# S4D convolution and gMLP on one core: stacked parameters in six rows, no tensor_scalar among them, the last inverse stage in four tiles, a new order

## The chip, the cores and the metric

The kernel runs on one core of one Trainium2 chip. The metric is the device time of one execution in microseconds (us). Smaller is better.

## The reference

```python
# u [1, 2048, 512]; A = -exp(log_A_real) + 1j*A_imag, C = C_real + 1j*C_imag: 512 channels x 128 modes
dt = exp(log_dt); P = exp((A * dt)[:, :, None] * arange(2048))
K = 2 * einsum("dn,dnl->dl", C * dt, P).real
y = irfft(rfft(layernorm(u), 4096) * rfft(K, 4096))[:2048]      # along the sequence
h = u + y + layernorm(u) * D_skip
z = gelu(layernorm(h) @ w_in)                                    # 512 -> 1792
z1, z2 = z[:, :896], layernorm(z[:, 896:])
out = h + (z1 * (w_sp @ z2 + b_sp[:, None])) @ w_out             # w_sp 2048 x 2048
```

## The kernel before

**Phase A** (0 to 302.7 us of the profiled execution) makes the convolution. `phase_a` writes its operations into a list (`Plan`): `RANKS` holds two digits in base 64 for each operation and so gives the order of issue, `FORMS` says which of two engines takes an operation that was written with `nc.either`, and `BANKS` names the PSUM bank of each intermediate. So the order on PE, DVE (VectorE), ACT, POOL (GpSimd) and on SP's DMA queue is a table, not the text. All operations of the list have one line in the profile, L252 (`Plan.issue`); they are told apart by their tiles.

The 512 channels go in four chunks of 128. `load_params` and `params(al, c0, n, rt)` make the discretised parameters, for the chunks 0, 1 and then 2 and 3 together: |C_imag| and |C_real|, the angle by Arctan and Sin, three phase terms that are split into a high part and a remainder (the low part), all in the tile `trio` (later `big`), with the PSUM bank `a` between. These six rows go to DRAM (`scr_stk`), from where `stack(c, h)` reads them back into `sw`, spread over 128 partitions so that a product with the constant `c_k` gives the phases. In `scr_stk` there are 16 rows a mode: the six rows at 0, the same six at 10, and four rows of ones between, which four DMAs (`marks`) write from `c_one` at the start. `table(c, h)` makes the decay tables `mt` on POOL (three multiplies, an Exp on ACT, a multiply by the weights). The eight `unit`s of a chunk turn phases and tables into the kernel K in its first transform stage (`ps<-c_k,sw`, `f`, `wa`, `wb`, `ks`); `st1` and `piece_c` continue it. `norm_small` and `norm_x` are the layer norm of the input (BATCH_NORM_STATS2 on `big`); `piece_a`, `piece_b` and `exchange` transform it. `piece_d` (`ps<-big,a`) is the second stage of K's transform, followed on DVE by the multiplication with the spectrum (`trio<-ps,trio`); it goes in eight pieces of four 128-wide matmuls, each over all 32 of the last index. `piece_e` (`ps<-c_inv,trio`) is the first inverse stage, eight pieces, copied to `big`.

**Phase B1** (from 302.7) is written in order by hand (L901 to L964). `lines(n, ...)` is the last inverse stage for a quarter n of the channels, in groups of four lines into PSUM banks `y`: quarter 0 uses two 64x64 tiles of TensorE (L755), the others four (L763). `put_by` copies a group to SBUF (`stash`, L775), `add` adds it to the residual `xq` (from PSUM for quarter 0, L783; from `stash` otherwise, L780). `moments` takes statistics (L787), `centre` and `spread` combine them over partitions by small products with `c_mean` (`lnh_pm` L796, `lnh_pv` L810), `root` is 1/sqrt on DVE (L815 to L824). `by_halves` (L863) normalises and transposes the first quarter into `ht` in two halves; `column` (L877) is the product with w_in, for quarter 0 first over a first half of the rows (A), then over the second (B).

**Phases B2 and B3** make z2's layer norm, the product with w_sp in seven products in the manner of Strassen, the gate and w_out.

## Time and profile before

| | us |
|---|---|
| median of three runs (lowest, highest) | 851.99 (851.52, 867.98) |
| the profiled execution | 850.38 |
| its span | 848.4 |
| mean granted TensorE clock in it | 0.990 |
| PE busy | 772.8 (91%) |
| DVE busy | 620.0 (73%) |
| ACT busy | 449.1 (53%) |
| POOL busy | 281.5 (33%) |

PE is the time of matmuls, PEld that of loading their weights, which overlaps it. A row of a timeline gives the start, the length, the engine (a q behind it: its queue of DMAs), the line, the operation, output<-inputs with shapes and types, and how many were drawn together; in brackets the idle time before it and what ended that. The columns of the table by stretches stand with the prediction.

### The profile page before, as it was taken

The numbers are of one execution on the slowest core, as the hardware profiler recorded it, in microseconds if no ns is written. First come the engines' busy times: TensorE is split into PE (matmuls) and PEld (weight loads), VectorE is DVE, ScalarE is ACT, GpSimd is POOL, SyncE is SP. The second block draws the span as 40 slices with busy tenths as digits, with TensorE's granted clock in tenths as the row PEclk, the third lists the DMA queues.
The fourth block names the chain that finished last, engine by engine and source line by source line (L and its number), as shares of the span: only waits on it lengthen the run. The fifth ranks groups of instructions, "written<-read, shape, count | busy, mean of one in ns | idle before, by whom it ended". The sixth has DMA issues, their size and how long they took to land.

```text
span 848.4 us, 19968 instructions
## 1 busy us (share of the span) xinstructions
PE 772.8 (91%) x8081; PEld 658.5 (78%) x8081; DVE 620.0 (73%) x1187; ACT 449.1 (53%) x785; POOL 281.5 (33%) x334
## 2 busy tenths in 40 slices
...
GB/s 234 142 144 120 123 88 133 84 78 40 127 3 208 278 97 127 132 143 149 88 146 127 1 124 123 190 237 210 195 207 210 167 148 187 155 234 232 185 107 79
DMA packets 73515, 123.14 MB, mean 145 GB/s; under 512 B 6864, under 2 KB 29520, under 8 KB 72144
## 3 DMA queue, kind: packets, MB, share of 16 engines
...
q14 instruction: 28, 0.23, 0.1%
...
## 4 chain that ended last, share of the span: by engine, by line
PE 63%; ACT 2%; DVE 1%; issue 0%; DVEq 0%; ACTq 0%
PE m L1197 33%; PE pz L992 9%; PE pz L887 8%; PE po L1120 7%; PE pl L1120 2%; PE ps L252 2%; PE y L763 1%; PE y L755 1%; ACT w1r L835 1%; ACT ht L844 0%; ACT stash L775 0%; PE lnh_pv L810 0%; PE lnh_pm L796 0%; DVE w1r L842 0%; DVE w1r L833 0%
## 5 line engine op out<-in xcount | busy, mean ns | idle before, releaser
L1197 PE MATMUL m<-wts,zc_wa 128*128 128x512 f32 x700 | 221.1, 395 | 0.0
L1197 PEld LDWEIGHTS m<-wts,zc_wa 128*128 128x128 f32 x700 | 131.7, 188 | 31.0
L1197 PE MATMUL m<-wts,zc_wb 128*128 128x512 f32 x350 | 138.0, 394 | 0.0
L1068 POOL DMA_DIRECT2D raws<-in_w_sp_dram x64 | 58.1, 1010 | 214.0 <-DMA raws<-in_w_sp_dram 212.5
L252 POOL TENSOR_TENSOR wa<-mt 128x512 f32<-128x512 f32 x96 | 106.5, 1129 | 34.3 <-PE ps L252 23.4
L687 ACT CAST wts<-raws 128x512 fp32r<-128x512 f32 x112 | 68.8, 619 | 47.3 <-DMA raws<-in_w_sp_dram 21.0
L688 DVE TENSOR_TENSOR wts<-raws,wts 128x512 fp32r<-128x512 f32 x112 | 77.2, 691 | 18.7 <-ACT wts L687 18.3
L1197 PEld LDWEIGHTS m<-wts,zc_wb 128*128 128x128 f32 x350 | 65.8, 188 | 15.6
L992 PE MATMUL pz<-w,ht 128*128 128x448 f32 x384 | 77.0, 362 | 0.0
L887 PE MATMUL pz<-ht,w1h 128*128 128x512 f32 (+1 forms) x248 | 74.4, 379 | 1.8 <-ACT ht L844 1.6
L992 PEld LDWEIGHTS pz<-w,ht 128*128 128x128 f32 x384 | 72.0, 187 | 4.9
L998 POOL TENSOR_SCALAR sm<-sm 128x1 f32<-128x1 f32 x16 | 5.5, 346 | 191.5 <-DVE sm L997 191.5
L252 PE MATMUL ps<-c_inv,trio 128*128 128x128 f32 x512 | 62.3, 284 | 4.2 <-DVE trio L252 3.4
L252 PEld LDWEIGHTS ps<-c_inv,trio 128*128 128x128 f32 x512 | 60.6, 198 | 5.8 <-DVE trio L252 3.6
L1120 PE MATMUL po<-w,gz 128*128 128x512 f32 x252 | 61.7, 392 | 0.0
L687 ACT CAST zc_wa<-raws 128x384 fp32r<-128x384 f32 (+1 forms) x70 | 37.1, 533 | 46.1 <-DVE raws L1102 26.3
L252 PE MATMUL ps<-big,a 128*128 128x128 f32 x448 | 56.4, 281 | 1.5 <-ACT big L252 0.8
L1120 PEld LDWEIGHTS po<-w,gz 128*128 128x128 f32 x252 | 47.3, 188 | 10.7
L252 PEld LDWEIGHTS ps<-big,a 128*128 128x128 f32 x448 | 52.1, 191 | 3.5 <-ACT big L252 0.9
L887 PEld LDWEIGHTS pz<-ht,w1h 128*128 128x128 f32 x248 | 45.7, 191 | 11.6 <-ACT ht L844 2.4
L252 DVE TENSOR_TENSOR f<-ps,wa 128x512 f32<-128x512 f32 (+1 forms) x64 | 46.4, 751 | 10.3 <-ACT ps L252 8.3
L687 ACT CAST zc_wa<-z 128x128 fp32r<-128x128 f32 (+2 forms) x56 | 23.7, 431 | 43.0 <-PE m L1197 35.9
...
## 6 DMA issues: line engine op xcount, KB each, us to landing
raws<-in_w_sp_dram SPq DMA_DIRECT2D x112, 256.0 KB, 4.2
...
```

What stands on the lines that cost most here:

```text
L252: r = getattr(getattr(self.nc, e), method)(*map(self.real, args), **{k: self.real(x) for k, x in kw.items()})
L687: nc.scalar.copy(hi, src)
L688: nc.vector.tensor_sub(lo, src, hi.bitcast(F32))
L755: nc.tensor.matmul(ys[n, g][w, i, :], gs[n][w, l, r], qv[w, r, l], start=(r == 0), stop=(r == 1), tile_position=(64 * h, 64 * h))
L763: nc.tensor.matmul(ys[n, g][o:o + 64, i, :], gs[n][w, l, r], qv[w, r, 16 * n + l], start=(r == 0), stop=(r == 1), tile_position=(64 * h, o))
L835: nc.scalar.activation(o, x, AF.Identity, bias=nmr[:, j:j + 1], scale=rstd[:, j:j + 1])
L887: nc.tensor.matmul(pt[:, w], a[:, q, f], ht[n][k][:, q, w], start=((q, i) == terms[0]), stop=((q, i) == terms[-1]))
L992: nc.tensor.matmul(pt[:, :FQ], a[:, q], w2[:, b, q, f], start=(q == 0 and i == 0), stop=(q == 3 and i == 2))
L998: nc.gpsimd.tensor_scalar_add(sm[:, 14:15], sm[:, 13:14], 1e-5)
L1068: nc.gpsimd.dma_start(r, ws[1], accum_op=ALU.add)
L1120: nc.tensor.matmul(pt, gz[fb][x][:, P * a:P * a + P], wo[:, y, fb, w], start=(first and fb == fbs[0] and i == 0), stop=(last and fb == fbs ...
L1197: nc.tensor.matmul(pt, x[:, f], y, start=(k == 0 and i == 0), stop=(k == KT - 1 and i == 2))
```

## The change

- **Stack.** `scr_stk` keeps six rows a mode; each half chunk is written once. `stack` loads these six rows twice, to partitions 0 to 47 and 80 to 127 of `sw`, 4 KB contiguous to a partition. The ones are set once in SBUF, on 32 to 95, ahead of the loads; the DMAs of `c_one` go. `c_k`, the channel order of the inputs and the tables' order follow the new layout; the three multiplies of a table are 816, 816 and 544 wide instead of 748, 714 and 714.
- **Parameters.** |x| is max(-x, x) by scalar_tensor_tensor instead of a bit mask by tensor_scalar; the two sign steps become scalar_tensor_tensor with an operand in PSUM and lose one operation; the scaling by 2 dt goes to ACT; a Sin on one element stands ahead of Arctan.
- **piece_d** of the last chunk goes in two halves of the last index, four pieces of eight half-wide matmuls each.
- **lines(0)** uses four tiles, as the others; `add(0, g)` then is two additions on 64 partitions. The adds and moments go by pairs of groups.
- **B1's order**: `lines(2, 2, 3)` before `spread(0)`; `lines(3, 2, 3)` before `by_halves`; the copies of quarter 2 split around `by_halves`' first half, those of quarter 3 all behind it; the three A columns together.
- **RANKS, FORMS, BANKS** are new throughout.

How the order moves, in three places. First SP's queue and POOL at the start (`trio`, `big`: parameters and input; `mt`: tables). SP before, from the second load of parameters on:

```order
L252 DMA trio<-in_par_dram 128x385
L252 DMA big<-in_u_a_dram 128x1024 x2
L252 DMA scr_stk<-in_c_one_dram 128x512 x3
L252 DMA scr_stk<-trio 64x768 x4
L252 DMA sw_89<-scr_stk 128x8x128
L252 DMA big<-in_par_dram 128x770
```

and now, where the ones are gone, the writes are two, and the 2 MB constant `a_78` stands behind the first load of `sw`:

```order
L251 DMA trio<-in_par_dram 128x385
L251 DMA big<-in_u_a_dram 128x1024 x2
L251 DMA scr_stk<-trio 64x6x128 x2
L251 DMA c_inv<-in_c_inv_dram 128x256
L251 DMA sw_89<-scr_stk 48x1024 x2
L251 DMA a_78<-in_c_a_dram 128x4096
L251 DMA wb<-in_c_f_dram 128x256
```

POOL before, from its first multiply to the weights of the first table (`trio<-trio` are the low parts and the products of weights):

```order
L252 TENSOR_TENSOR trio<-trio 128x128 x2
L252 TENSOR_TENSOR mt_91<-wb 128x748
L252 TENSOR_TENSOR trio<-trio 128x128
L252 TENSOR_TENSOR mt_91<-wb 128x714
L252 TENSOR_TENSOR trio<-trio 128x128 x2
L252 TENSOR_TENSOR mt_91<-wb 128x714
L252 DMA c_k<-in_c_k_dram 128x1024
L252 TENSOR_TENSOR mt_92<-wb 128x714
L252 TENSOR_TENSOR mt_92<-wb 128x748
L252 TENSOR_TENSOR mt_91<-mt_91,wb 128x64x4
```

and now, with three table multiplies ahead of the first low part and two more ahead of `c_k`:

```order
L251 TENSOR_TENSOR mt_92<-wb 128x816
L251 TENSOR_TENSOR mt_91<-wb 128x544
L251 TENSOR_TENSOR mt_91<-wb 128x816
L251 TENSOR_TENSOR trio<-trio 128x128 x3
L251 TENSOR_TENSOR mt_91<-wb 128x816
L251 TENSOR_TENSOR mt_92<-wb 128x816
L251 DMA c_k<-in_c_k_dram 128x1024
L251 TENSOR_TENSOR trio<-trio 128x128 x3
L251 TENSOR_TENSOR mt_92<-wb 128x544
L251 TENSOR_TENSOR mt_91<-mt_91,wb 128x64x4
```

Five table multiplies instead of three now stand ahead of the last triple of `trio` operations, and the load of `c_k` between them.

Second, TensorE at the end of phase A, from the last phase product of the last chunk's units to the inverse stage (`ks`: st1; `f`, `wa`: units; `a_78`: piece_d). Before:

```order
L252 MATMUL ps_101<-wa,wb 32x64 x16
L252 MATMUL ps_99<-wb,ks_80 64x2x32 x16
L252 MATMUL ps_98<-wb,ks_81 64x2x32 x16
L252 MATMUL ps_100<-big,a_78 128x2x2x32 x4
L252 MATMUL ps_101<-big,a_78 128x2x2x32 x4
L252 MATMUL ps_97<-big,a_78 128x2x2x32 x4
L252 MATMUL ps_99<-big,a_78 128x2x2x32 x4
L252 MATMUL ps_100<-big,a_78 128x2x2x32 x4
L252 MATMUL ps_98<-big,a_78 128x2x2x32 x4
L252 MATMUL ps_101<-big,a_78 128x2x2x32 x4
L252 MATMUL ps_100<-big,a_78 128x2x2x32 x4
L252 MATMUL ps_101<-c_inv,trio 128x128 x8
```

and now, where the first piece stands among the last units and the second behind the last `f` and `wa`:

```order
L251 MATMUL ps_100<-big,a_78 128x2x2x16 x8
L251 MATMUL ps_98<-wb,ks_85 64x2x32 x16
L251 MATMUL ps_99<-wb,ks_81 64x2x32 x16
L251 MATMUL ps_97<-f_93 32x64 x16
L251 MATMUL ps_97<-wa,wb 32x64 x16
L251 MATMUL ps_101<-big,a_78 128x2x2x16 x8
L251 MATMUL ps_97<-wb,ks_84 64x2x32 x16
L251 MATMUL ps_99<-wb,ks_80 64x2x32 x16
L251 MATMUL ps_98<-big,a_78 128x2x2x16 x8
L251 MATMUL ps_97<-big,a_78 128x2x2x16 x8
L251 MATMUL ps_99<-big,a_78 128x2x2x16 x8
L251 MATMUL ps_98<-big,a_78 128x2x2x16 x8
```

All eight pieces came behind the last `ks` before; now two come ahead of it, and six half-wide ones follow.

Third, DVE and ACT in phase B1. DVE before, from the first add (`y_0` to `y_3`: the groups of quarter 0) to the first statistic:

```order
L783 TENSOR_TENSOR xq_3684<-y_0_3848,xq_3684 128x512
L787 BN_STATS stats<-xq_3684 128x6 x4
L783 TENSOR_TENSOR xq_3684<-y_1_3849,xq_3684 128x512
L787 BN_STATS stats<-xq_3684 128x6 x4
L783 TENSOR_TENSOR xq_3684<-y_2_3882,xq_3684 128x512
L787 BN_STATS stats<-xq_3684 128x6 x4
L783 TENSOR_TENSOR xq_3684<-y_3_3883,xq_3684 128x512
L787 BN_STATS stats<-xq_3684 128x6 x4
L801 TENSOR_TENSOR small<-stats,lnh_pm 128x32
```

and now, with two additions to a group and the moments behind a pair:

```order
L776 TENSOR_TENSOR xq_3700<-y_0_3881,xq_3700 64x4x128 x2
L776 TENSOR_TENSOR xq_3700<-y_1_3882,xq_3700 64x4x128 x2
L780 BN_STATS stats<-xq_3700 128x6 x8
L776 TENSOR_TENSOR xq_3700<-y_2_3915,xq_3700 64x4x128 x2
L776 TENSOR_TENSOR xq_3700<-y_3_3916,xq_3700 64x4x128 x2
L780 BN_STATS stats<-xq_3700 128x6 x8
L794 TENSOR_TENSOR small<-stats,lnh_pm 128x32
```

The moments moved behind the second group of their pair, and the four additions became eight.

ACT before, from the first normalised lines (`w1r`, `ht`) to the last copies (`stash_3843` is quarter 2, `stash_3844` quarter 3):

```order
L835 ACTIVATE w1r<-xq_3684,small 128x128 x3
L844 CAST ht_4071<-w1r 128x4x128 x2
L775 COPY stash_3843<-y_0_4023 64x4x128 x2
L775 COPY stash_3843<-y_1_4024 64x4x128 x2
L835 ACTIVATE w1r<-xq_3684,small 128x128 x4
L844 CAST ht_4071<-w1r 128x4x128 x2
L775 COPY stash_3843<-y_2_4073 64x4x128 x2
L775 COPY stash_3843<-y_3_4074 64x4x128 x2
L775 COPY stash_3844<-y_0_4107 64x4x128 x2
L775 COPY stash_3844<-y_1_4108 64x4x128 x2
L775 COPY stash_3844<-y_2_4208 64x4x128 x2
L775 COPY stash_3844<-y_3_4209 64x4x128 x2
```

and now (`stash_3876` is quarter 2, `stash_3877` quarter 3), with half of quarter 2 ahead of the normalised lines and nothing of quarter 3 between:

```order
L766 COPY stash_3876<-y_0_4060 64x4x128 x2
L766 COPY stash_3876<-y_1_4061 64x4x128 x2
L828 ACTIVATE w1r<-xq_3700,small 128x128 x3
L837 CAST ht_4142<-w1r 128x4x128 x2
L766 COPY stash_3876<-y_2_4095 64x4x128 x2
L766 COPY stash_3876<-y_3_4096 64x4x128 x2
L828 ACTIVATE w1r<-xq_3700,small 128x128 x4
L837 CAST ht_4142<-w1r 128x4x128 x2
L766 COPY stash_3877<-y_0_4148 64x4x128 x2
L766 COPY stash_3877<-y_1_4149 64x4x128 x2
L766 COPY stash_3877<-y_2_4182 64x4x128 x2
L766 COPY stash_3877<-y_3_4183 64x4x128 x2
```

One pair of quarter 2's copies moved ahead of the first half of quarter 0, and quarter 3's copies all stand behind both halves, with no `lines` left that waits for them.

The diff, with the tables cut to a first line:

```diff
@@ -38,31 +38,31 @@
 RANKS = (
-    "02030Q0g1r001b1a1Z0O0b0c0d181M1X1Y1D4G3f4-3h0I010B0D0E0F0H0J0K0M0R0T0U0V0W0Z0S0e0h080k0t0u10111B090C0A0G0L0N0P0q0Y0s0+0-"
+    "0I000F0g1r0O0i0o0p1H1L1n1o0w2l1M2Z2L0805040302010607090A0B0C0D0E0G0H0K0N0R0T0Q0V0Y0X0J0x0y0z1E1G1T0L0U0S0a0k0l2i0+100-1B"
...
@@ -113 +113 @@
-    ck = np.zeros((8, 16, 2, 2, 8, 32))
+    ck = np.zeros((16, 8, 2, 2, 8, 32))
@@ -115 +115 @@
-        a = ck[i, :, :, :, i]
+        a = ck[:, i, :, :, i]
@@ -122 +121,0 @@
-    c["c_one"] = np.ones((1, 4 * NS))
@@ -288 +287 @@
-    c_lt, c_f, dpad, half_pi, magic, dummy, dts, ndt = (wb(n) for n in (34, 256, P, 1, 1, 1, NCH, NCH))
+    c_lt, c_f, dpad, half_pi, magic, dummy, dts, ndt, dt2 = (wb(n) for n in (34, 256, P, 1, 1, 1, NCH, NCH, NCH))
@@ -318,3 +316,0 @@
-    marks = stk_d.rearrange("c h p r n -> (c h p) r n")[:, 6:10]
-    for c in range(NCH):
-        nc.sync.dma_start(marks[P * c:P * c + P], cst["c_one"].rearrange("o (r n) -> o r n", r=4).to_broadcast([P, 4, NS]))
@@ -330,0 +327,3 @@
+    for h in range(2):
+        for o in (32, 64):
+            nc.either(lambda: nc.vector.memset(sws[h][o:o + 32], 1.0), lambda: nc.gpsimd.memset(sws[h][o:o + 32], 1.0))
@@ -333,0 +333 @@
+    nc.vector.tensor_scalar_mul(dt2, dts, 2.0)
@@ -418 +418 @@
-        nc.vector.tensor_scalar(b.bitcast(I32), ci.bitcast(I32), 0x7FFFFFFF, None, op0=ALU.bitwise_and)
+        nc.vector.scalar_tensor_tensor(b, ci, -1.0, ci, op0=ALU.mult, op1=ALU.max)
@@ -428 +428 @@
-        nc.vector.tensor_scalar(a.bitcast(I32), cr.bitcast(I32), 0x7FFFFFFF, None, op0=ALU.bitwise_and)
+        nc.vector.scalar_tensor_tensor(a, cr, -1.0, cr, op0=ALU.mult, op1=ALU.max)
@@ -433,0 +434 @@
+        nc.scalar.activation(dummy, half_pi, AF.Sin)
@@ -439,6 +440,5 @@
-        nc.scalar.activation(a, a, AF.Abs)
-        nc.vector.tensor_scalar(b, cr, 0.0, 2.0, op0=ALU.is_lt, op1=ALU.mult)
-        nc.vector.tensor_sub(a, b, a)
-        nc.scalar.activation(a, a, AF.Abs)
-        nc.vector.tensor_scalar(b, ci, 0.0, 0.5, op0=ALU.is_lt, op1=ALU.mult)
-        nc.vector.scalar_tensor_tensor(a, b, -0.25, a, op0=ALU.add, op1=ALU.mult)
+        nc.scalar.activation(a, a, AF.Abs, scale=0.5)
+        nc.vector.scalar_tensor_tensor(a, cr, 0.0, a, op0=ALU.is_lt, op1=ALU.subtract)
+        nc.scalar.activation(a, a, AF.Abs, scale=0.5)
+        nc.vector.scalar_tensor_tensor(b, ci, 0.0, a, op0=ALU.is_lt, op1=ALU.mult)
+        nc.vector.scalar_tensor_tensor(a, b, 2.0, a, op0=ALU.mult, op1=ALU.subtract)
@@ -460,2 +460 @@
-                for r in (0, 10):
-                    nc.sync.dma_start(stk_d[c0 + c, h, :, r:r + 6], st6[64 * h:64 * h + 64, :, c, :])
+                nc.sync.dma_start(stk_d[c0 + c, h].rearrange("r p n -> p r n"), st6[64 * h:64 * h + 64, :, c, :])
@@ -467 +466 @@
-            nc.vector.tensor_scalar(mx[:, w], co[:, w], dts[:, c0 + c:c0 + c + 1], 2.0, op0=ALU.mult, op1=ALU.mult)
+            nc.scalar.activation(mx[:, w], co[:, w], AF.Identity, scale=dt2[:, c0 + c:c0 + c + 1])
@@ -473 +472,2 @@
-        nc.sync.dma_start(sws[h], stk_d[c, h].rearrange("(s a i) r n -> (i r) s a n", s=4, a=2))
+        for o in (0, 80):
+            nc.sync.dma_start(sws[h][o:o + 48].rearrange("p s a n -> p (s a n)"), stk_d[c, h].rearrange("r (i x) n -> (r i) (x n)", i=8))
@@ -477,4 +477,5 @@
-        rc = rcs[:, c].rearrange("p i s -> p (i s)")
-        for lo, n in ((0, 22), (22, 21), (43, 21)):
-            nc.gpsimd.tensor_tensor(mt[:, lo:lo + n], rc[:, 64 * h + lo:64 * h + lo + n].unsqueeze(2).to_broadcast([P, n, 34]),
-                                    c_lt.unsqueeze(1).to_broadcast([P, n, 34]), op=ALU.mult)
+        mv = mt.rearrange("p (x i) k -> p x i k", i=8)
+        rc, w = (rcs[:, c, k, 64 * h:64 * h + 64].rearrange("p (i x) -> p x i", i=8) for k in range(2))
+        for lo, n in ((0, 3), (3, 3), (6, 2)):
+            nc.gpsimd.tensor_tensor(mv[:, lo:lo + n], rc[:, lo:lo + n].unsqueeze(3).to_broadcast([P, n, 8, 34]),
+                                    c_lt.unsqueeze(1).unsqueeze(1).to_broadcast([P, n, 8, 34]), op=ALU.mult)
@@ -482,2 +483 @@
-        nc.gpsimd.tensor_tensor(mt[:, :, 30:], mt[:, :, 30:],
-                                rc[:, P + 64 * h:P + 64 * h + 64].unsqueeze(2).to_broadcast([P, 64, 4]), op=ALU.mult)
+        nc.gpsimd.tensor_tensor(mv[:, :, :, 30:], mv[:, :, :, 30:], w.unsqueeze(3).to_broadcast([P, 8, 8, 4]), op=ALU.mult)
@@ -659,2 +659,3 @@
-        for g in range(8):
-            piece_d(c, g, 0, 32)
+        for lo, n in ((0, 32),) if c + 1 < NCH else ((0, 16), (16, 16)):
+            for g in range(n // 4):
+                piece_d(c, g, lo, n)
@@ -748,10 +748,0 @@
-        if n == 0:
-            for turn in range(2):
-                for i in range(4):
-                    for r in range(2):
-                        for x, g in enumerate(groups):
-                            h, l = turn ^ x, 4 * g + i
-                            w = slice(64 * h, 64 * h + 64)
-                            nc.tensor.matmul(ys[n, g][w, i, :], gs[n][w, l, r], qv[w, r, l], start=(r == 0), stop=(r == 1),
-                                             tile_position=(64 * h, 64 * h))
-            return
@@ -782,2 +773,4 @@
-            v = v.rearrange("p l (d x) -> p l d x", d=4)
-            nc.vector.tensor_add(v, ys[n, g].rearrange("p l (x d) -> p l d x", d=4), v)
+            h, y = g % 2, ys[n, g].rearrange("p l (x d) -> p l d x", d=4)
+            v = xqs[n % 3][:, 4 * (g - h):4 * (g - h) + 8].rearrange("p l (d x) -> p l d x", d=4)[64 * h:64 * h + 64]
+            for odd in range(2):
+                nc.vector.tensor_add(v[:, odd::2], y[64 * odd:64 * odd + 64], v[:, odd::2])
@@ -872,2 +865,2 @@
-                put_by(2, 0)
-                put_by(2, 1)
+                put_by(2, 2)
+                put_by(2, 3)
@@ -897,4 +889,0 @@
-    def both(n, g):
-        add(n, g)
-        moments(n, g)
-
@@ -908,2 +897,4 @@
-        for g in range(4):
-            both(0, g)
+        for g in range(0, 4, 2):
+            for f in add, moments:
+                f(0, g)
+                f(0, g + 1)
@@ -915 +905,0 @@
-        root(0, spread(0))
@@ -916,0 +907,3 @@
+        root(0, spread(0))
+        put_by(2, 0)
+        put_by(2, 1)
@@ -917,0 +911 @@
+        lines(3, 2, 3)
@@ -920,8 +914,4 @@
-        for n, g in ((2, 2), (2, 3), (3, 0), (3, 1)):
-            put_by(n, g)
-        column(0, 0, A)
-        column(0, 1, A)
-        lines(3, 2, 3)
-        column(0, 2, A)
-        put_by(3, 2)
-        put_by(3, 3)
+        for g in range(4):
+            put_by(3, g)
+        for fb in range(3):
+            column(0, fb, A)
@@ -1265 +1255,2 @@
-        return x.reshape(4, 4, NCH, 8, -1).transpose(2, 3, 0, 1, 4).reshape(NCH, P, -1)
+        y = x.reshape(4, 4, NCH, 8, -1).transpose(2, 3, 0, 1, 4)
+        return y.reshape(NCH, 2, 8, 8, -1).transpose(0, 1, 3, 2, 4).reshape(NCH, P, -1)
@@ -1293 +1284 @@
-           (("xhat", [P, 16, 4, NL2]), ("stk", [NCH, 2, 64, 16, NS]), ("h", [L, D]), ("z1", [4, FB, P, 512]))}
+           (("xhat", [P, 16, 4, NL2]), ("stk", [NCH, 2, 6, 64, NS]), ("h", [L, D]), ("z1", [4, FB, P, 512]))}
```

More of the change, by code (lines that the diff above doesn't have):

```diff
@@ new lines @@
+    "3s4x453y443Q4u4J3f3b4X3H734K6t4L2F3O2w222T3S302K2f1x213F2y3C2V3I2C233J2B2r2m3P3E3W3R343M3L2e3K2o3X3Y3g3h3l3+3m3v3w3x3-41"
+    "474A4E4G4Q4R4V4b4p514q525d5P4e726P6v4y5E4i6q4+5s534s6T5t4v4h5q4d4c6A5L4n546k624f4g5I4t5w7l7C768W8d1k1m2G2X2t3d3u481p1-20"
+    "2D2M2bBd2j2q2z3Z3n3o494H4U4W4k4o5Q5u4O4P696B6C6D3T42434S6d6n4N4-675v6G6H6o6-775J5o5c6F6L6MHm6e6f6g6h6y6z70797A7B7I7J9K9f"
+    "8UAY969UAZC3AdEk9c9-A0AlBBBGClFJFK6J6K6Q6R5N5O686E5S5V5y5-6N6O5k5r6m6u6p6w82837r7s7j7q7X7Z7a7b7V7W84852v3D3j4F4T4j4B4I4m"
@@ new lines @@
+    "4l564r575T6+7d7e2W2c2S353V3i3k3t46404Y4C4Z506I8T8b5G5H5K5U5W5X5Y5Z5a5b5n5j60666i7x7z4M4z5B4w5859555A5D5C5e5R5h5m8n9B9I7t"
+    "7w7P7Y7c7k8E6S656X6U6V6W6Y6Z6a6b6s6c6x717+9F9L5M5l5i5x5z615f5g5+5p6j636l6r8B8e8f7T7m7g7R7S7U7Q7f7n7o7y7p87888Z97987L7O8A"
+    "7K7M7N7u7v868C8J8D8S8i8s9495999x819C9R9Z9o898G787D7G7H8o8t8M8N7h7i74757E7F8w9DAqAr8u939k9l9J9YACAU9s9tAsAt9uABAMAc9N9jA8"
+    "AG9g9nATAX9e9m9M9WBPBQCdCpCICQBiC8C9CABfBgCMCUCGCHCeE08H8X8O7-808F8K8Q8I8a8Y8P8j8k8r8vA9AgAh8L8g8m8R8V8c8q8l8y8p91909S92"
@@ L69 @@
-    "21021400342234213412441303303344314"
+    "214403231041444344421200002243344330242014220400140201121110141223002012001341034334302413143434433143204412421131102420"
+    "431034021012110001243431143423431342304343314422132044220100240013213420441212112104443124330213201223423041441033210420"
+    "30023400301040213320243121044330112"
 )
@@ L914, in phase_b1 @@
         add(1, 0)
+        lines(2, 2, 3)
         root(0, spread(0))
-        lines(2, 2, 3)
+        put_by(2, 0)
+        put_by(2, 1)
         lines(3, 0, 1)
+        lines(3, 2, 3)
         by_halves(0)
         load_x(3)
-        for n, g in ((2, 2), (2, 3), (3, 0), (3, 1)):
-            put_by(n, g)
-        column(0, 0, A)
-        column(0, 1, A)
-        lines(3, 2, 3)
-        column(0, 2, A)
-        put_by(3, 2)
-        put_by(3, 3)
+        for g in range(4):
+            put_by(3, g)
+        for fb in range(3):
+            column(0, fb, A)
         for g in range(1, 4):
```

42 lines of the change are left out of this document (16 added, 26 removed).

## The prediction

> **What bounds the kernel now.** I read the table of engine busy time by stretches first, then the chain that ended last, then the timelines of single engines where TensorE stands idle. In the table the columns are the stretch, its length, the busy time of PE, PEld, DVE, ACT and POOL (with instructions), the granted clock, the DMA share and GB/s.
>
> ```profile
> PE 63%; ACT 2%; DVE 1%; issue 0%; DVEq 0%; ACTq 0%
> 20.00:40.00 20.00, 4.17 (x12) 3.02 (x12) 19.65 (x55) 11.21 (x26) 13.99 (x15) 1.00 0.52 169
> 40.00:140.00 100.00, 78.44 (x2040) 64.76 (x2043) 83.37 (x134) 83.47 (x138) 80.11 (x92) 0.98 0.42 120
> 260.00:274.00 14.00, 8.92 (x420) 7.20 (x420) 9.64 (x13) 10.18 (x16) 9.04 (x13) 1.00 0.84 220
> 274.00:303.00 29.00, 24.36 (x198) 23.60 (x200) 15.84 (x16) 6.03 (x9) 0.00 (x0) 0.94 0.56 229
> 303.00:322.00 19.00, 17.35 (x458) 16.71 (x454) 12.50 (x44) 8.59 (x16) 0.00 (x0) 1.00 0.45 113
> 322.00:339.00 17.00, 13.82 (x141) 13.12 (x140) 9.04 (x28) 13.27 (x25) 0.00 (x0) 0.80 0.56 145
> 339.00:412.00 73.00, 72.88 (x323) 58.98 (x323) 42.35 (x126) 36.15 (x74) 0.00 (x0) 1.00 0.47 147
> 412.00:848.00 436.00, 432.52 (x1940) 361.41 (x1938) 319.00 (x578) 176.51 (x340) 83.52 (x112) 1.00 0.67 160
> ```
>
> From 339 on TensorE is busy 505.4 of 509 us, and the change touches nothing there: what comes earlier at 339 comes earlier at the end, one for one. Between 20 and 40 VectorE is the bound (19.65 of 20), between 40 and 140 no engine is (TensorE idles 21.6 us), and in the four stretches from 260 to 339 TensorE idles 5.1, 4.6, 1.7 and 3.2. The change works in three of these places.
>
> **The change, part one: the start.** The parameters of the first chunk go through VectorE, while POOL fills the exponent tables; the phases (the product of c_k with sw) wait for both and for a round trip through DRAM.
>
> ```profile
> 7.08 0.23 DVE L252 TENSOR_SCALAR trio<-trio 128x128 int32<-128x128 int32 x1 [6.18 <-DMA trio<-in_par_dram]
> 14.00 1.47 DVE L252 TENSOR_SCALAR trio<-trio,wb 128x128 f32<-128x128 f32 x1
> 16.76 0.20 DVE L252 TENSOR_SCALAR trio<-trio 128x128 f32<-128x128 f32 x1
> 21.53 6.70 DVE L252 TENSOR_SCALAR trio<-trio 128x128 int32<-128x128 int32 x1
> 35.15 1.13 DVE L252 TENSOR_SCALAR trio<-trio 128x128 f32<-128x128 f32 x1
> 21.52 2.80 POOL L252 TENSOR_TENSOR mt<-wb 128x714 f32<-128x714 f32 x2
> 24.27 0.64 POOL L252 TENSOR_TENSOR mt<-mt,wb 128x256 f32<-128x256 f32 x1
> 24.87 3.27 POOL L252 TENSOR_TENSOR wa<-mt 128x512 f32<-128x512 f32 x3
> ```
>
> The same 128x128 operation takes 0.23 us at 7.08, when POOL is idle, and 6.70 at 21.53. That one ends at 28.23, just as a row of six POOL operations ends (24.87 + 3.27 = 28.14) that began with it. VectorE stood 6.70 - 0.23 = 6.47 us behind one instruction, in the stretch that VectorE bounds. Replacing it by an operation without that wait returns 6.5. The other two slow ones return 1.47 - 0.20 = 1.3 and 1.13 - 0.20 = 0.9, so the most that this part gives on VectorE is about 9; I allow 10.
>
> The trace has no operation in that place with two inputs from SBUF and the multiply-and-maximum form; its nearest rows are additions of two SBUF operands, with POOL idle and with POOL busy.
>
> ```profile
> 190.48 0.68 DVE L252 TENSOR_TENSOR wb<-wb,wa 128x512 f32<-128x512 f32 x1
> 259.72 1.49 DVE L252 TENSOR_TENSOR wb<-wb,wa 128x512 f32<-128x512 f32 x1
> 259.51 1.15 POOL L252 TENSOR_TENSOR wa<-mt 128x512 f32<-128x512 f32 x1 [0.23 <-PE ps L252]
> ```
>
> At 259.72 the addition ends with the one POOL operation that was running (260.66), 0.8 us late, and not with the next, which follows at once. So two SBUF inputs can wait too, but here for one operation and not for a burst. The new |x| operations read one tensor twice; there are six, two to a call of params. I take 0.2 to 1.1 us for a wait and expect few of the six to meet one. The Trainium skill, page "SBUF — State Buffer", section "SBUF: two separate sides", speaks against this edit: VectorE and GpSimd share a port pair as an exclusive lock, which a VectorE operation in a two-port mode takes, and also one with two SBUF inputs, for the whole instruction. The trace agrees that both kinds wait (6.70 and 1.49 us); it shows no burst waited out by the second kind. By the page alone the gain of this part would be zero and the sum six microseconds less.
>
> On the other side of the start stands the stack:
>
> ```profile
> 18.37 2.03 SPq L252 DMA_DIRECT2D scr_stk<-in_c_one_dram  x3
> 20.50 4.49 SPq L252 DMA_DIRECT2D scr_stk<-trio  x4
> 31.28 0.39 SPq L252 DMA_DIRECT2D sw<-scr_stk  x1
> 18.59 0.87 POOL L252 TENSOR_TENSOR trio<-trio 128x128 f32<-128x128 f32 x2
> 35.48 2.04 PE L252 MATMUL ps<-c_k,sw 128*128 128x512 f32 x4 [4.42 <-DMA sw<-scr_stk]
> ```
>
> The low parts are ready at 19.46; SP is then still issuing the ones (to 20.40), and its four writes take until 24.99. Without the ones and with two writes that is 0.9 + 2.2 = 3.1 sooner. The load moves the same bytes in 4 KB runs instead of 512 B runs, with a landing time that I put between 3.0 and the 4.2 seen (35.48 - 31.28). Against it, POOL now has five table multiplies before the last low parts, where it had three: two more by 1.4 to 1.6 us, some 3 later. Together the first phase product comes at 28 to 32 instead of 35.48. SP's 2 MB load of a2 now follows the first load of sw; at the 169 GB/s of that stretch it lasts 12 us, which is what already lay between the first and the second load of sw. Both roads, VectorE's and the stack's, give about the same, and neither can give much without the other. **Term one: -6, between -10 and 0.** The activations that take the scaling over, the early table load and the memsets fall where ACT (11.21 of 20) and VectorE before 7.08 have room; uncovered they cost under 1 us, within the bounds.
>
> **Part two: the end of the transform.** The last chunk's 32 matmuls (64 records) become 64 (128 records) of half the width, in eight pieces; two of them go ahead of the last units. The last row below is from the chain (start, length, what).
>
> ```profile
> 273.86 7.75 PE L252 MATMUL ps<-big,a 128*128 128x128 f32 x64 [0.76 <-ACT big L252]
> 276.92 8.01 DVE L252 TENSOR_TENSOR trio<-ps,trio 128x1024 f32<-128x1024 f32 x7 [0.63 <-PE ps L252]
> 284.98 14.40 PE L252 MATMUL ps<-c_inv,trio 128*128 128x128 f32 x112 [3.37 <-DVE trio L252]
> 299.98 2.05 PE L252 MATMUL ps<-c_inv,trio 128*128 128x128 f32 x16 [0.60 <-DVE big L252]
> 338.73 0.35 PE lnh_pm L796 x4
> ```
>
> Today 273.86 to 284.98 (11.1 us) passes until the inverse can begin, 3.37 of it waiting for VectorE's last multiply. After the change the first four inverse steps need only the first half's products, which are done by then, so that wait goes. A half-wide record lies between 88 ns (0.35 / 4, the narrowest here) and 121 ns (7.75 / 64, the full width); six pieces are 96 records, 8.4 to 11.6 us, the middle 10. That is 1.1 less than 11.1, and the wait of 0.60 goes too: -1.7. The two early pieces (2.8 to 3.9 us of TensorE) lie in its 5.1 idle us between 260 and 274; uncovered they cost up to 1 us over the bound, covered well they bring the last units forward. **Term two: -2, between -5 and +1.**
>
> **Part three: the last inverse stage.** Times below are after its first matmul, 302.70.
>
> ```profile
> 302.70 7.09 PE L755 MATMUL y<-big,g 64*64 64x128 f32 x125 [0.68 <-ACT big L252]
> 306.45 0.69 DVE L783 TENSOR_TENSOR xq<-y,xq 128x512 f32<-128x512 f32 x1 [4.93 <-PE y L755]
> 312.17 0.87 DVE L787 BATCH_NORM_STATS2 stats<-xq 128x6 f32<-128x128 f32 x4
> 313.88 1.98 PE L763 MATMUL y<-big,g 64*64 64x128 f32 x64
> 315.79 0.62 PE L810 MATMUL lnh_pv<-small,c_mean 128*128 128x16 f32 x4
> 321.71 0.39 PE L887 MATMUL pz<-ht,w1h 128*128 128x256 f32 x1 [1.65 <-ACT ht L844]
> 326.39 1.45 DVE L848 TENSOR_TENSOR ht<-w1r,ht 128x512 fp32r<-128x512 f32 x2
> 328.37 3.68 PE L763 MATMUL y<-big,g 64*64 64x128 f32 x60 [3.18 <-ACT stash L775]
> 337.02 0.40 PE L887 MATMUL pz<-ht,w1h 128*128 128x256 f32 x2
> 338.56 0.51 PE L796 MATMUL lnh_pm<-stats,c_mean 128*128 128x16 f32 x4
> ```
>
> In four tiles a pair of groups takes 1.98 instead of 3.5, so the first add can begin at 2.0, not 3.75. But there are eight adds on 64 partitions, each still 512 long: 8 x 0.6 + 16 x 0.22 + gaps = 8.4, to 10.4. Before, the last moments ended at 312.17 + 0.87, which is 10.3. TensorE's gain is eaten by VectorE. Then spread's product stands behind one more pair of lines: its end moves from 13.7 to 15.2, and the first half-column from 19.0 to 20.5. That is the cost of the new order. Its gain: the three first half-columns now run together, 4.3 us (12 matmuls at 0.12 each, from the row at 337.02 and its neighbours), to 24.8; the 3.18 us of waiting for the stash and the 3.68 of the last lines are gone from between them; the second halves are ready at 26.6 (25.1 before, plus 1.5), three more half-columns end at 30.9. The next statistic (338.56, at 35.9 before) comes near 31.7: -4.2. TensorE will idle 3 to 4 us ahead of the first half-column, though, and after the 3.18 of before 60 matmuls took 3.68, twice as long as 64 at 313.88, with a granted clock of 0.80 in that stretch; the cost of such a slow piece on what follows is up to 1.9. **Term three: -3.5, between -4.5 and -2.**
>
> **The sum.** -6 - 2 - 3.5 = -11.5 against the profiled execution's 850.38 (span 848.4) gives 838.9. The median of the runs shown is 1.6 above that execution, so the forecast is **840.5 us**.
>
> **The rivals.** *A: the |x| operations wait as the old ones did.* Six waits of one POOL operation (1.1) are 6.6, as much as the 6.5 removed; term one is zero and the time 846.5. For it: the row at 259.72. Against it: an operation that waits for one of POOL's and not for six costs little where POOL has gaps. 0.22. (The rule of the page named above would make it this one.)
> *B: the new order closes part of TensorE's 21.6 idle us between 40 and 140.* Each instruction there has a new place, and VectorE, ACT and POOL are at 80 to 83 of 100, so a third (8 us) could go: 832.5. Against it: POOL's table work is the same there, and three engines at four fifths, each waiting on the others, leave little. 0.18.
> *S, slower: the |x| operations starve behind whole bursts of POOL*, as the one at 21.53. Three of the six, one to a call, at 6.5 each, are 19.5 where one such stall stood: term one turns from -6 to +13, 859.5. It decides from two stalls of over 3 us on. Against it is the 259.72 row, which let go after one operation. 0.08.
>
> **How the numbers follow.** My forecast has 0.52. Its own bounds are -19.5 and -1, so 832.5 to 851. The range reaches down to 829, since B has its half there, and up to 852, which holds A and leaves S out. A measurement of this kernel tells about 2% from no change, 17 us: below 835.0 is faster, above 869.0 slower. Faster: most of B (0.15) and a sixth of the forecast (0.09), 0.24. Slower: only the far end of S, 0.03. Within: 0.73.
>
> **What would show it.** Right: no VectorE operation of over 2 us before 35; the first phase product near 30; 20 to 40 with TensorE over 6 us busy; no wait for VectorE ahead of the first c_inv product of the last chunk; the last moments of the first adds about 10.4 after the first y matmul, and the second lnh_pm (338.56 now) 31 to 33 after it instead of 35.9, with the wait for the stash gone. Wrong: a scalar_tensor_tensor of several us in the parameters (A or S), the first phase product at 34 or later, or the first y matmul earlier than 294 by more than what 20 to 40 and 274 to 303 explain (B).

## The result

The changed kernel takes 850.25 us (median of 20 executions, 842.14 to 858.42) beside 853.34 for the kernel before on the same chips; the ratio is 0.9946, interval [0.9922, 0.9970], some 4.6 us less (it leaves out the slowest executions). In a second set (r1, below) it was 0.9984 [0.9953, 1.0016], a difference that can't be told from none. The forecast was 840.5, a gain of 11.5 us: the time lies in the range that was given, but the gain is less than half of the sum.

The times fall along with the granted clock: of the 20, the three with a mean clock of 0.988 or more took 842.1 to 844.3 us, the seven with 0.973 or less 852.3 to 858.4. The executions with the highest clock are near the forecast; most are not. The profile shown here is r1's, of the same kernel: an execution of 856.70 us, span 854.9, clock 0.974. It is longer than the median, and 6.5 us longer than the profiled execution of the kernel before, so it shows the loss near its largest. (The profiled execution of the first set, 856.65 us, has the same 96 records in 20.75 us and its first y matmul at 312.82.) The table by stretches (columns as in the prediction):

```profile
20.00:40.00 20.00, 8.49 (x48) 5.41 (x52) 19.80 (x80) 18.52 (x44) 17.61 (x24) 1.00 0.61 202
40.00:140.00 100.00, 89.09 (x2394) 75.76 (x2387) 87.47 (x115) 89.19 (x146) 89.99 (x98) 0.97 0.30 78
255.00:260.00 5.00, 2.72 (x66) 2.62 (x65) 0.00 (x0) 0.86 (x2) 0.21 (x1) 0.85 1.00 351
260.00:265.00 5.00, 3.88 (x72) 3.39 (x71) 0.00 (x0) 1.09 (x2) 0.00 (x0) 0.50 1.02 423
265.00:285.00 20.00, 19.87 (x93) 19.87 (x94) 4.90 (x4) 0.08 (x1) 0.00 (x0) 0.50 0.42 170
```

TensorE is busy 8.5 us between 20 and 40 instead of 4.2, and 89 of the next 100 instead of 78. Then, from 265 to 285, it is busy all but 0.13 us at half the clock. The timeline of TensorE, from the first phase product on to the last inverse stage:

```profile
26.29 1.19 PE L251 MATMUL ps<-c_k,sw 128*128 128x512 f32 x2 [3.35 <-DMA sw<-scr_stk]
251.37 1.97 PE L251 MATMUL ps<-big,a 128*128 128x64 f32 x16 [1.03 <-DVE big L251]
254.36 0.32 PE L251 MATMUL ps<-f 128*32 128x64 f32 x8
257.28 0.54 PE L251 MATMUL ps<-f 128*32 128x64 f32 x24 [2.60 <-issue]
258.20 3.41 PE L251 MATMUL ps<-big,a 128*128 128x64 f32 x16
265.13 20.74 PE L251 MATMUL ps<-big,a 128*128 128x64 f32 x96 [0.68 <-ACT big L251]
285.67 7.29 PE L251 MATMUL ps<-c_inv,trio 128*128 128x128 f32 x48
295.52 7.25 PE L251 MATMUL ps<-c_inv,trio 128*128 128x128 f32 x48 [2.56 <-DVE trio L251]
306.02 5.47 PE L251 MATMUL ps<-c_inv,trio 128*128 128x128 f32 x32 [3.24 <-DVE big L251]
312.85 4.37 PE L754 MATMUL y<-big,g 64*64 64x128 f32 x148 [1.36 <-ACT big L251]
```

The first phase product stands at 26.29 instead of 35.48. The first early piece takes 123 ns a record (1.97 / 16); after a stall of 2.60 us that nothing in the profile explains, the second takes 213, and the other 96 records 216 each. The first y matmul, 28.8 us behind the late piece_d before, is 47.7 us behind it now. Not all of the 18.9 between is in the records: 96 in 20.74 us instead of 64 in 7.75 make 13.0. The rest is in the inverse stage. No wait stands ahead of its first product any more, but two new ones stand inside, 2.56 for VectorE's multiplies and 3.24 for its copies, where 3.37 and 0.60 stood before, and its products take 20.0 us instead of 16.5. From the second lnh_pm on (338.56 before, 345.16 now) the two kernels are alike: to the end of the span it is 509.8 and 509.7 us.

At the start, SP's queue shows where the 9.2 us lie:

```profile
18.50 1.37 SPq L251 DMA_DIRECT2D scr_stk<-trio  x2
22.26 0.81 SPq L251 DMA_DIRECT2D sw<-scr_stk  x2
```

The writes are issued by 19.87 instead of 24.99, and the load of sw goes out at 22.26 instead of 31.28, 9.0 us sooner. The first phase product follows that load by 4.0 us, before by 4.2, so the landing itself gained next to nothing.

| stage, us of the profiled execution | before | changed (r1) | r5, old tail | r7, and Abs on ACT |
|---|---|---|---|---|
| to the first phase product | 35.5 | 26.3 | 26.5 | 26.4 |
| to the first piece_d behind the last unit | 238.4 | 238.8 | 231.6 | 224.4 |
| to the first y matmul | 28.8 | 47.7 | 32.1 | 34.6 |
| to the second lnh_pm | 35.9 | 32.3 | 33.9 | 35.2 |
| to the end | 509.8 | 509.7 | 509.8 | 509.9 |

### The profile page after: what moved, and what is told of

Its sections match the earlier page's. It is cut to its first block, busy times and chain, and to the rows that moved or that the text cites. A ratio compares the mean times of both kernels' runs of the same rounds, so it can differ in the third digit from the quotient of the medians.

```text
span 854.9 us, 20107 instructions
## 1 busy us (share of the span) xinstructions
PE 790.9 (93%) x8145; PEld 674.4 (79%) x8145; DVE 612.4 (72%) x1176; ACT 448.8 (52%) x796; POOL 286.7 (34%) x340
## 4 chain that ended last, share of the span: by engine, by line
PE 84%; DVE 8%; ACT 5%; issue 2%; DMA 1%; SPq 0%; ACTq 0%; DVEq 0%
PE m L1187 33%; PE ps L251 25%; PE pz L982 9%; PE pz L880 7%; PE po L1110 7%; PE pl L1110 2%; DVE trio L251 2%; ACT big L251 2%; DVE f L251 1%; DVE ps L251 1%; DVE big L251 1%; DVE stats L780 1%; ACT ps L251 1%; DVE wa L251 1%; PE y L754 1%
## 5 line engine op out<-in xcount | busy, mean ns | idle before, releaser
L251 PE MATMUL ps<-big,a 128*128 128x128 f32 (+1 forms) x512 | 74.6, 311 | 3.1 <-DVE big L251 1.0
L251 PEld LDWEIGHTS ps<-big,a 128*128 128x128 f32 x512 | 71.0, 222 | 6.4 <-issue 1.3
L251 PE MATMUL ps<-c_inv,trio 128*128 128x128 f32 x512 | 65.6, 291 | 5.8 <-DVE big L251 3.2
L251 PEld LDWEIGHTS ps<-c_inv,trio 128*128 128x128 f32 x512 | 63.1, 205 | 7.4 <-DVE big L251 3.4
L251 DVE TENSOR_TENSOR trio<-ps,trio 128x1024 f32<-128x1024 f32 (+1 forms) x34 | 38.5, 1162 | 31.2 <-PE ps L251 27.5
L251 ACT COPY big<-ps 128x512 f32<-128x512 f32 x49 | 28.1, 588 | 58.1 <-PE ps L251 57.7
```

The source lines that it names most:

```text
L251: r = getattr(getattr(self.nc, e), method)(*map(self.real, args), **{k: self.real(x) for k, x in kw.items()})
```

## The experiments

**Theory 1** is that the clock takes the gain: half-wide records hold it down. **Theory 2** is that the gains were smaller than forecast. Later ones stand with their runs.

**r1: the changed kernel again.**

> The changed kernel again, for a profile of an execution whose clock was not halved, and for more times. Theory 1 (the clock): the three gains are there, some 10 us, and what takes half of them back is a granted clock of 0.5 over the half-wide piece_d matmuls in part of the executions; so an execution at a mean clock of 0.99 takes 841 to 843 us, one at 0.97 takes 855 to 858, and in the profile the 96 half-wide records after the last unit take 11.5 us (120 ns each) at full clock or 20 us (216 ns) at half. Theory 2 (the gains are smaller than forecast): at full clock it takes 846 or more.

854.23 us in the median (844.98 to 858.60); the execution at a clock of 0.992 took 844.98, those at 0.972 to 0.976 took 852.8 to 858.6. The 96 records took 20.74 us. Theory 1's split by clock is there; the profile did not catch an execution at full clock.

**r3: only the division, in the kernel before.**

```diff
-        for g in range(8):
-            piece_d(c, g, 0, 32)
+        for lo, n in ((0, 32),) if c + 1 < NCH else ((0, 16), (16, 16)):
+            for g in range(n // 4):
+                piece_d(c, g, lo, n)
```

> The kernel before with only piece_d of the last chunk in two halves of the last index, in its old order. Theory 1: 128 records at 120 ns are 15.4 us instead of 7.75, the inverse starts without its wait of 3.4, so 0 to 5 us slower at full clock and up to 12 where the clock is low. Theory 2: 0 to 2 us faster, the division hides VectorE's multiplies.

866.73 us in the median, ratio 1.0111 [1.0069, 1.0153]: 9.5 us slower by the ratio. Its profiled execution had the full clock, 1.00 in every stretch of 5 us from 279 to 294:

```profile
279.07 14.51 PE L252 MATMUL ps<-big,a 128*128 128x64 f32 x128 [0.76 <-ACT big L252]
294.89 14.40 PE L252 MATMUL ps<-c_inv,trio 128*128 128x128 f32 x112 [1.32 <-DVE trio L252]
312.61 7.09 PE L756 MATMUL y<-big,g 64*64 64x128 f32 x125 [0.68 <-ACT big L252]
```

113 ns a record at full clock, against 121 at full width: half the columns cost nearly as much. Half-wide records that begin at full clock also keep it. The wait for VectorE falls from 3.37 to 1.32, which pays 2.0 of the 6.8 us lost. Two executions, at clocks of 0.988 and 0.991, took 860.1 and 858.6 us; the four at 0.967 to 0.976 took 865.9 to 876.6.

**r8 and r9: the division and the clock.** Both put 40 copies of a dead buffer on ACT ahead of the last copy that piece_d needs; r8 is divided, r9 not.

```diff
+        if c + 1 == NCH and s == 7:
+            e["pre"] = [lambda: tc.nc.scalar.copy(kss[3], kss[2])] * 40
```

> The kernel before with piece_d of the last chunk in halves (as in r3), and 40 copies of a dead buffer on ACT ahead of the last copy that piece_d waits for, so that TensorE stands idle some 10 us and its clock is low when the half-wide records begin; the copies only cost time. Theory 1 (half-wide records do not raise the clock again): all 128 records at about 216 ns, 26 to 28 us at a granted clock of 0.5. Rival (any steady work raises it after some us): 4 to 5 us slow, then 113 ns each, 17 to 18 us in all.

> The counterpart of the run with halves and idle: the kernel before, undivided, with the same 40 copies on ACT ahead of the last copy that piece_d waits for. Theory 1 (the width decides whether the clock comes back): the 64 full-width records begin at a clock of 0.5 and reach full speed after 3 to 5 us, 9 to 11 us in all, and most of the run's extra time is the idle itself. Rival (any long idle keeps the clock low for what follows): 64 records at 216 ns or more, 14 us.

Of r8, TensorE's timeline:

```profile
289.10 27.57 PE L254 MATMUL ps<-big,a 128*128 128x64 f32 x128 [13.68 <-ACT big L254]
```

and two rows of its table by stretches (0.50 in all stretches between as well):

```profile
290.00:295.00 5.00, 5.00 (x26) 5.00 (x25) 1.23 (x1) 0.00 (x0) 0.00 (x0) 0.50 0.01 3
320.00:325.00 5.00, 5.00 (x30) 5.00 (x29) 1.42 (x2) 3.10 (x4) 0.00 (x0) 0.61 0.18 72
```

The same two views of r9:

```profile
291.33 10.03 PE L254 MATMUL ps<-big,a 128*128 128x128 f32 x64 [13.66 <-ACT big L254]
```

```profile
290.00:295.00 5.00, 3.67 (x17) 3.67 (x18) 1.22 (x1) 1.25 (x3) 0.00 (x0) 0.50 0.31 127
295.00:300.00 5.00, 5.00 (x41) 4.97 (x40) 3.34 (x3) 0.00 (x0) 0.00 (x0) 0.89 0.00 0
```

With the same idle, full-width records bring the clock back within 5 us and the 64 take 10.0 instead of 7.75; half-wide ones stay at 0.50 for all 27.6 us (215 ns each), and it rises only under the c_inv products behind them. From piece_d's first record to the first y matmul it is 47.8 us in r8 and 29.5 in r9 (y at 336.89 and 320.86): begun at the low clock, the division costs 18.3 us. The whole executions took 884.57 (r8) and 868.02 (r9), one of each.

The undivided kernels among the runs below show the same without the copies. In r7 the 64 records begin at 250.78 at the low clock and take 9.64 us; two stretches of it:

```profile
250.00:255.00 5.00, 4.31 (x24) 4.22 (x21) 1.23 (x1) 0.58 (x1) 0.00 (x0) 0.52 1.01 419
255.00:260.00 5.00, 5.00 (x44) 4.81 (x43) 4.28 (x4) 0.00 (x0) 0.00 (x0) 1.00 1.00 409
```

In r2, r6 and r11 they take 10.23, 9.58 and 9.53. So the clock is often low at this place, whatever the width; the width decides whether that costs some 2 us, or 13 (the changed kernel) to 20 (r8).

**r2: undivided, in the changed order.** The two early pieces are moved behind the last unit. In this kernel the first inverse products do not wait for the last of the multiplies, so its time is a bound only.

```diff
+        for g in range(8):
+            piece_d(c, g, 0, 32)
...
+            x[i]["rank"] = x[2]["rank"] - 0.9 + 0.2 * i + 0.1 * k
```

> The changed kernel with piece_d of the last chunk undivided: eight pieces of four full-width matmuls, all behind the last unit. Theory 1: 64 records in 7.8 us as before the change and no long stretch at clock 0.5, so times near 841 with little spread, 6 to 10 us under the median of the changed kernel. Theory 2: the division is worth its 2 us, and this kernel is 0 to 4 us slower than the changed one. Theory 3 (the loads of the next phase now begin while the units still run and starve TensorE's instruction stream): the idle 2.6 us ahead of the last units and the low clock behind it stay, and the time is within 3 us of the changed kernel's.

842.7 us, ratio 0.987 [0.9843, 0.9897], all four executions between 841.4 and 843.2. Its first inverse product starts at 271.03, while three of the multiplies come only from 276.70 on. From piece_d to the first y matmul it takes 36.4 us, beside 34.5 and 34.6 in r6 and r7, which also begin at the low clock but have the old order of the inverse stage: the new order is no gain. r5 has every wait in place.

**r10: the early pieces held back**, divided as changed, with a dependency on the last unit.

```diff
+    for o in early:
+        o["rank"] = 1258 + o["rank"] / 4096
+        o["after"] = next(x for x in nc.ops if x["rank"] == 1258)
```

> The changed kernel with the two early half-wide pieces held back behind the last unit; division, order of the multiplies and of the inverse stage as changed. If the early pieces are what lowers the clock (they stretch the end of the units, and TensorE's stall falls there): first piece_d near 259, all 128 records at full clock in 14 to 15 us in most executions, 3 to 8 us under the changed kernel. If the clock falls anyway: 128 records at 216 ns, 27 us, and the time as changed or slower.

855.52 us, ratio 1.0019 [0.9993, 1.0045]: no better.

```profile
255.19 2.78 PE L251 MATMUL ps<-big,a 128*128 128x64 f32 x23 [0.70 <-ACT big L251]
259.61 21.84 PE L251 MATMUL ps<-big,a 128*128 128x64 f32 x105 [1.64 <-issue]
```

piece_d begins 10 us earlier than in the changed kernel (265.13), but now holds all 128 records, and 105 of them take 208 ns. The first y matmul, at 308.37 instead of 312.85, keeps 4.5 us of it in this profile, which is of r10's fastest execution; the median keeps nothing. The early pieces, with the stall, delay the units; they are not what holds the clock down.

**r13: the next phase's loads held.** The stall of 2.60 us falls when these loads begin.

```diff
+    for r in [*loads, load_x(2)]:
+        tc.add_manual_dep(r.ins, rest.hold.name, info, reason="after the units")
```

> The changed kernel with the loads of the next phase (three of xq, two of g, four of w1r) held until TensorE's last product of the units, some 6 us later than now; nothing else changed. If these loads are what holds TensorE up at the end of the units (2.60 us in which it waits for nothing that the profile shows, while the DMA engines are at a share of 1.0) and so lowers the clock ahead of the half-wide records: no such stall ahead of the last f and wa products, the 96 records of piece_d at 110 to 120 ns instead of 216, and 842 to 847 us in most executions. If the clock falls all the same: records at 216 ns and within 3 us of the changed kernel.

Three executions of four took 854.9 to 855.0 us, one, at a clock of 0.990, 839.98. The profile (853.1, clock 0.978), TensorE's timeline and then the stretch of the stall:

```profile
257.06 0.87 PE L251 MATMUL ps<-f 128*32 128x64 f32 x24 [2.33 <-issue]
265.01 20.75 PE L251 MATMUL ps<-big,a 128*128 128x64 f32 x96 [0.70 <-ACT big L251]
```

```profile
255.00:260.00 5.00, 2.94 (x62) 2.77 (x62) 0.00 (x0) 0.86 (x2) 0.21 (x1) 0.64 0.17 36
```

The DMA share at the place is 0.17 instead of 1.00 and the stall is there all the same, behind the same eight records. The loads are not its cause; what is stays open, and with it what first lowers the clock. The same kernel at a mean clock of 0.990 and at 0.974 to 0.978 differs by 15 us.

**r5: the old tail.** The changed kernel, with piece_d of the last chunk undivided and piece_d and piece_e in the kernel before's order, engines and banks.

```diff
-        for lo, n in ((0, 32),) if c + 1 < NCH else ((0, 16), (16, 16)):
-            for g in range(n // 4):
-                piece_d(c, g, lo, n)
+        for g in range(8):
+            piece_d(c, g, 0, 32)
...
+    for i, o in enumerate(tail):
+        o["rank"] = 4096 + i
```

> The changed kernel, whose last chunk has piece_d undivided and piece_d and piece_e in the order, on the engines and in the banks of the kernel before. Theory 1 (the start gains 9 us and the units some 5 more; the divided piece_d and the order of the first inverse stage behind it lose them again): the first piece_d near 259.5, the first y matmul 29 to 32 us behind it, and a time of 834 to 839 us, 1.4 to 2.2% under the kernel before. Theory 2 (the division itself is good, and the earlier run without it was fast only because its inverse stage did not wait for the last products): 843 us or more.

837.43 us beside 850.73, ratio 0.9819 [0.9774, 0.9864]: by the ratio 15.4 us under the kernel before, three times the change's own gain.

```profile
258.11 2.83 PE L252 MATMUL ps<-big,a 128*128 128x128 f32 x23 [0.69 <-ACT big L252]
261.73 5.19 PE L252 MATMUL ps<-big,a 128*128 128x128 f32 x41 [0.78 <-issue]
290.21 7.22 PE L765 MATMUL y<-big,g 64*64 64x128 f32 x256 [1.43 <-issue]
```

The first piece_d behind the units stands 7 us earlier than in the changed kernel (the early pieces' 5.4 and most of the stall), and it reaches the y stage in 32.1 us instead of 47.7. r5 takes back the division and the new order of the inverse stage together.

**r6, r7 and r12: |x|.** r6 is r5 with the bit mask again; r7 is r5 with Abs on ACT; r12 is the kernel before with Abs on ACT.

```diff
-        nc.vector.scalar_tensor_tensor(b, ci, -1.0, ci, op0=ALU.mult, op1=ALU.max)
+        nc.scalar.activation(b, ci, AF.Abs)
...
-        nc.vector.scalar_tensor_tensor(a, cr, -1.0, cr, op0=ALU.mult, op1=ALU.max)
+        nc.scalar.activation(a, cr, AF.Abs)
```

> The run before (old tail) with |x| made by the bit mask of tensor_scalar again, everything else as changed. Theory L (both forms wait for POOL's bursts; the start gains by the order and by the stack, not by the form): within 1.5 us of the run with scalar_tensor_tensor. Theory F (my forecast: the form saves the stall): 3 to 7 us slower, with the first phase product 3 us later or more.

> The run with the old tail, with |x| made by ACT's Abs, so that no engine shares anything with POOL for it. If VectorE bounds the start, the two waits of the changed kernel (2.66 and 4.1 us instead of 0.29 and 0.42) come back as 2 to 6 us. If the stack's way or ACT bounds it, within 1.5 us of the run with the old tail.

> The kernel before with only |x| moved to ACT's Abs: no VectorE operation of 6.70 us at 21.53. My forecast's first term alone (VectorE bounds the start): 3 to 7 us faster, first phase product still near 35 as the stack's way is unchanged. If the stack's way decides: within 1.5 us of the kernel before.

r6: 837.47 us, ratio 0.9814 [0.9756, 0.9872], as r5. r7: 830.13 us, ratio 0.9730 [0.9679, 0.9781], 7.3 us less than r5. r12: 850.84 beside 853.27, ratio 0.9977 [0.9948, 1.0006], no difference that can be told. The changed kernel's two slow |x| operations beside POOL's, in r1's timelines:

```profile
17.05 2.67 DVE L251 SCALAR_TENSOR_TENSOR ps<-trio 128x128 f32<-128x128 f32 x1
17.19 1.28 POOL L251 TENSOR_TENSOR trio<-trio 128x128 f32<-128x128 f32 x3
18.43 1.12 POOL L251 TENSOR_TENSOR mt<-wb 128x544 f32<-128x544 f32 x1
44.85 4.10 DVE L251 SCALAR_TENSOR_TENSOR big<-big 128x256 f32<-128x256 f32 x1
44.28 4.38 POOL L251 TENSOR_TENSOR wa<-mt 128x512 f32<-128x512 f32 x4
```

and the other one of the larger size (busy us, mean ns of one, idle before):

```profile
L251 DVE SCALAR_TENSOR_TENSOR ps<-big 128x256 f32<-128x256 f32 x1 | 0.4, 422 | 0.0
```

Both waits end with a whole row of POOL operations, as the 6.70 did. This one, at 52.33, took 0.42, though POOL was at work then too (one operation to 52.39, the next from 52.37). r6's mask operations in the two slow places, and POOL's row beside the second:

```profile
16.55 3.00 DVE L252 TENSOR_SCALAR trio<-trio 128x128 int32<-128x128 int32 x1
16.91 2.84 DVE L252 TENSOR_SCALAR ps<-trio 128x128 int32<-128x128 int32 x1
44.85 0.72 DVE L252 TENSOR_SCALAR big<-big 128x256 int32<-128x256 int32 x1
44.29 5.49 POOL L252 TENSOR_TENSOR wa<-mt 128x512 f32<-128x512 f32 x5
```

In the first place the mask waits as long as the new form. In the second it is through after the first operation of POOL's row, where the new form waits for four (4.10). r6 gains by it, TensorE being busy 93.4 us between 40 and 140 instead of 88.3 in r5 and the first piece_d coming 2.6 us sooner, and loses as much behind it, where it has more low clock (9.58 us instead of 8.8 for piece_d's 64 records; 6.18 instead of 5.29 for the 128 records behind the first lnh_pm). The times are equal: the change's |x| saved nothing. r7 has neither wait; its first piece_d comes 224.4 us behind the first phase product, r5's 231.6. Between 40 and 140:

```profile
40.00:140.00 100.00, 93.97 (x2524) 80.53 (x2527) 88.35 (x120) 92.84 (x152) 95.02 (x104) 1.00 0.31 80
```

In r12 the stall at 21.53 is gone too. But Abs stands in ACT's queue behind other work, the first parameters are 2.0 us later (RECIPROCAL at 11.15, before 9.18), the stack's load goes out later (33.90, before 31.28), and the first phase product with it:

```profile
33.90 0.39 SPq L252 DMA_DIRECT2D sw<-scr_stk  x1
37.99 2.90 PE L252 MATMUL ps<-c_k,sw 128*128 128x512 f32 x6 [10.01 <-DMA sw<-scr_stk]
```

There the stack's way decides, not VectorE's stall. Of the start's 9.2 us, then, none is shown to come from the form of |x| (26.3 us to the first phase product in r6, 26.5 in r5); the stack, the new order and the other edits of the parameters share it, and these runs do not part them.

**r4 and r11: phase B1.** r4 is the kernel before with only B1 changed. r11 is r7 with one line moved:

```diff
-        centre(0)
         lines(2, 0, 1)
+        centre(0)
```

> The kernel before with only phase B1 changed: lines(0) in four tiles, the additions in eight, the new order of lines, copies and columns. Forecast and theory 1: 2 to 4.5 us faster, the second lnh_pm 31 to 33 us after the first y matmul instead of 35.9. Theory 2: no gain here, within 1.5 us of the kernel before.

> The run with the old tail and |x| on ACT, and the first product with c_mean put behind the lines of quarter 2's first pair, so that TensorE does not idle 3.9 us ahead of it. If the low clock behind that idle is what eats the gain of the new order there: the next 128 records of lines near 3.7 us instead of 6, the second lnh_pm 32 to 33 us after the first y matmul instead of 35, and 1.5 to 2.5 us less than the run without. If not: within 1 us of it.

r4: 854.22 beside 854.92 us, ratio 0.9998 [0.9973, 1.0023]: nothing.

```profile
317.81 1.04 PE L788 MATMUL lnh_pm<-stats,c_mean 128*128 128x16 f32 x4 [3.71 <-DVE stats L779]
318.77 6.49 PE L753 MATMUL y<-big,g 64*64 64x128 f32 x128
342.22 0.62 PE L788 MATMUL lnh_pm<-stats,c_mean 128*128 128x16 f32 x4 [0.60 <-DVE stats L779]
```

TensorE idles 3.71 us ahead of the first statistic, and the 128 records behind it take 6.49 instead of 3.72; the second lnh_pm comes 35.5 us after the first y matmul (306.71). r11, with two lines in that idle:

```profile
297.62 0.62 PE L800 MATMUL lnh_pm<-stats,c_mean 128*128 128x16 f32 x4 [1.06 <-DVE stats L791]
298.17 1.98 PE L765 MATMUL y<-big,g 64*64 64x128 f32 x64
```

The next 64 records are at full speed, and the second lnh_pm comes at 30.6 (286.54 to 317.09) instead of 35.2 in r7. The time is 827.39 us, ratio 0.9708 [0.9670, 0.9747]. It was timed on another chip than r7 (0.9730), with the intervals overlapping: the profile shows the stage 4.7 us shorter, the times do not part the two kernels. It is the fastest kernel of this study.

## Why the prediction was wrong

- **Term one (-6): within its bounds by luck, wrong in its cause.** Measured -9.2, with none of it shown for the form of |x|. The landing that was put at 3.0 to 4.2 us took 4.0; the load itself went out 9.0 us sooner. The step "for one operation and not for a burst" failed: two of the six |x| operations waited out rows of four POOL operations, for 6.1 us in all (2.67 - 0.29 and 4.10 - 0.42), the other four took 0.3 to 0.5 us. S's bursts came true for these two, without S's time; A's six waits of one operation did not. (The addition at 259.72 does let go after one operation, but it does not end with it at 260.66: it ends at 261.21, and POOL's next operation started in between, at 260.62.) The Trainium skill, page "SBUF — State Buffer", section "SBUF: two separate sides", had said that two SBUF inputs take the shared lock too; the two slow rows agree, and the wait is longer than the one instruction that it names.
- **The units (0 in the sum).** r5 shows -6.8, of rival B's kind; the changed kernel shows +0.4, since the early pieces (5.4) and the stall (2.60) took it back. I had laid the early pieces into idle time, "uncovered they cost up to 1 us over the bound"; with the stall they cost more than their length. (A third of 21.6 us is 7.2, not the 8 of rival B.)
- **Term two (-2, at most +1): the step that failed.** "A half-wide record lies between 88 ns and 121 ns" was true at full clock (113) and left out the other: 216 at half clock, and half-wide records did not end it. At full clock the division costs 4.7 us from piece_d to the first y matmul (33.5 in r3, 28.8 before), begun at the low clock 18.3 (47.8 in r8, 29.5 in r9). In the changed kernel this stage is 18.9 longer. The step "so that wait goes", and the 0.60 with it, failed as well: 2.56 and 3.24 stand inside the inverse stage instead. So the division was a loss at either clock. I had seen the low clock in the y stage and priced it there, but did not ask what it would do to the records that I was making narrower. None of my rivals held it.
- **Term three (-3.5): the new time was right, the old one was not what it replaced.** Forecast 31.7 to the second lnh_pm, 32.3 in the profile:

```profile
323.93 0.62 PE L789 MATMUL lnh_pm<-stats,c_mean 128*128 128x16 f32 x4 [2.42 <-DVE stats L780]
324.48 3.72 PE L754 MATMUL y<-big,g 64*64 64x128 f32 x128
345.16 0.62 PE L789 MATMUL lnh_pm<-stats,c_mean 128*128 128x16 f32 x4 [0.61 <-DVE stats L780]
```

  But the 35.9 of before held 2.5 us of low clock, which the same stage of r3 does not have (33.4, from 312.61 to 345.96), as behind the same wait of 3.18:

```profile
338.27 1.96 PE L764 MATMUL y<-big,g 64*64 64x128 f32 x60 [3.18 <-ACT stash L776]
345.96 0.51 PE L797 MATMUL lnh_pm<-stats,c_mean 128*128 128x16 f32 x4
```

  These 60 records took 3.68 before. And the new order has an idle of its own (3.7 to 3.9 in r4, r5 and r7), behind which the next 128 records were slow each time, so that the stage is back at 33.9 to 35.5. In the profile above the idle was 2.42, and they took their 3.72. That VectorE's doubled adds would eat TensorE's gain was right.
- **The end** was right: 509.7 to 509.9 us in every column of the table. The whole is near the forecast only where the clock is high (842 to 844 beside 840.5). No profile caught such an execution; by the runs above the start's larger gain pays there for the division, so that this agreement is luck too.
